# The middle term of a three-term fp32 split: 20 of its tiles by TensorE and ScalarE instead of VectorE

## The chip, the cores and the metric

The kernel runs on one core of a Trainium2 chip. Time is device microseconds (us) of the whole execution. Six executions of the kernel before are at hand, and one more that was profiled. The engines are named as in the profile: PE (TensorE, matmul), PEld (its weight load), DVE (VectorE), ACT (ScalarE), POOL (GpSimd) and SP (SyncE, which issues most DMAs).

## What is computed

A retention layer over 768 steps, for 4 batches and 8 heads of width 64, and behind it two matrix products with a SiLU between them:

```python
# attention: q, k, v are (4, 8, 768, 64)
gamma = 1.0 - 2.0 ** (-5.0 - np.arange(H))
for t in range(S):
    state = gamma * state + einsum('bhd,bhe->bhde', k[:, :, t], v[:, :, t])
    y[:, :, t] = scale * einsum('bhd,bhde->bhe', q[:, :, t], state)
x = y.transpose(0, 2, 1, 3).reshape(3072, 512)
# w_in is (512, 2048), w_out is (2048, 512)
h = x @ w_in
g = h * (1.0 / (1.0 + np.exp(-h)))
return g @ w_out
```

The weights come as 64-bit floating point numbers; the kernel makes 32-bit numbers of their two words itself.

## The kernel before

**Precision by three products.** The large products run in the format fp32r, which the kernel treats as narrower than fp32. So each operand t is split in three parts, each a plane of one tile: plane 0 is the high part H, t scaled by slightly less than one (HALF) and rounded; plane 1 the low part L; plane 2 the middle M, a sum of H and L in which one is scaled by EPS = 2^-12 or its inverse. The product H·H' + L·L' goes into one PSUM bank (ha, or oa), M·M' into another (hb, or ob), and the difference of the two, with ha scaled by ONE_E, is the product in nearly full precision. One product of 128 x 512 thus takes three passes: `product_in` issues eight matmuls into ha, four into hb. The M plane is read by the last four only.

**Units, groups, slices.** Time is cut in six chunks c of 128 steps; a unit n is one chunk of one batch, so that there are 24 units and units 4c to 4c+3 make group c of 512 columns of x. w_in is used in 16 slices f of 128 columns. `product_in(c, f)` makes ha and hb of slice f and group c; ScalarE copies ha out (L492), VectorE takes hb off (L493, "g"), ScalarE does SiLU (L494), and the result goes to device memory to be fetched again for the second half, which multiplies by w_out (L617 to L619).

**Visits.** `visit(m)` works on three units at once: it transposes k and q of unit m (kp, qp, L331; ScalarE copies them out, L333), makes scores and state sums of unit m-1 (sc, L347 and L357; VectorE: am L365, mid L373, qt L322, state L377) and the output y of unit m-2 (L389). `finish_y` then copies y out (ys, L424) and `split_x` splits it: H on ScalarE (L435), L (L436) and M (L437) on VectorE. The last eight matmuls of y wait for a token that GpSimd writes (`fence`, L305), and once per chunk GpSimd also scales a table gq (L278), which qt reads.

**Weights.** `take_w` converts one slice: ScalarE ca (L193), VectorE five to six steps (cs L195, ca L197, cs L200, cp L202, cp L204, cs L207), and `split_w` makes H on ScalarE (L117), L on VectorE (wil, L119) and ScalarE (L121), and M on VectorE (L122).

**Order.** TensorE's order is written out by hand: visits 0 to 9 with products (0, 0) and (0, 1) after visits 6 and 9, then pairs of products (group 0 and group 1 with one slice) with visits 10 to 13 between them, then more products. On the other engines a scheduler chooses the order, from its own estimate of times, and every engine then runs its queue in that fixed order. Group 2 (LATE) is used twice: it is split at once into a tile of its own, kept in device memory too, and split again later by `late_x`. PSUM has three banks for ha, hb and kp, handed out in turn by `turn`:

```python
    def turn(name):
        turns[0] += 1
        return ps_h.tile([128, 512], FP32, tag=f"h{turns[0] % 3}", name=name)
```

so that each user of a bank waits for the reader of the bank's user three turns before.

Of the kernel before, what the change touches and what calls it, by code (L numbers as in the profile page):

```python
# [12 lines left out]
FP32 = mybir.dt.float32  # L13
FP32R = mybir.dt.float32r
U32 = mybir.dt.uint32
AF = mybir.ActivationFunctionType
ALU = mybir.AluOpType
# [8 lines left out]
EPS = 2.0 ** -12  # L26
# [5 lines left out]
def kernel(  # L32
# [27 lines left out]
    nc = tc.nc  # L60
    B, H, S, D = q.shape
    DM, DF = moe_w_in.shape
    C = 128
    NC = S // C
    HP = H // 2
# [7 lines left out]
    scale = 1.0 / math.sqrt(D)  # L73
# [4 lines left out]
    def pool(name, bufs, **kw):  # L78
        return ctx.enter_context(tc.tile_pool(name=name, bufs=bufs, **kw))
# [4 lines left out]
    const = pool("const", 1)  # L84
    ld = pool("ld", 2)
    one = pool("one", 1)
# [17 lines left out]
    def w_slot(f, name):  # L104
        if f < NF - 4:
            return wpool.tile([128, 3, 512], FP32R, tag=f"w{f}", name=f"{name}{f}")
        if f == NF - 4:
            quads[name] = wpool.tile([128, 4, 3, 512], FP32R, tag="wq", name=f"{name}4")
        return quads[name][:, f - NF + 4]

    def split_w(f, w32, name, factor):

        w = w_slot(f, name)
        lo = conv.tile([128, 512], FP32, tag="wl", name=f"{name}l_{f}")
        after = held if f >= NF - 4 else evac
        with tc.issue_after(after[0]) if after else ExitStack():
            nc.scalar.activation(out=w[:, 0, :], in_=w32, func=AF.Copy, scale=HALF * factor)  # L117
        high = w[:, 0, :].bitcast(FP32)
        nc.vector.scalar_tensor_tensor(out=lo, in0=w32, scalar=factor, in1=high,  # L119
                                       op0=ALU.mult, op1=ALU.subtract)  # L120
        nc.scalar.activation(out=w[:, 1, :], in_=lo, func=AF.Copy, scale=1.0 / EPS)  # L121
        nc.vector.scalar_tensor_tensor(out=w[:, 2, :], in0=high, scalar=EPS, in1=lo,  # L122
                                       op0=ALU.mult, op1=ALU.subtract)
        return w


    units = [(c, b) for c in range(NC) for b in range(B)]
# [103 lines left out]
            load_w(n // 2)  # L231


    ident = const.tile([128, 128], FP32, tag="ident", name="ident")
    make_identity(nc, ident)

    lag = const.tile([128, C], FP32, tag="lag", name="lag")
    for o in range(2):
        part = lag[ts(o, D), :D]
        nc.gpsimd.iota(part, pattern=[[1, D]], base=0, channel_multiplier=-1,  # L240
# [4 lines left out]
    for j in range(2):  # L245
        for a in range(HP):
            evac[:] = [nc.scalar.activation(out=decay[:, j, a, :], in_=lag[:, :D],
                                            func=AF.Exp, scale=float(lg[2 * a + j])).ins]
# [34 lines left out]
    xt, kt, qt, am = {}, {}, {}, {}  # L283
# [10 lines left out]
    turns = [0]  # L294
# [4 lines that stand above are left out]
# [18 lines left out]
    def scale_q(n):  # L317
        c, b = units[n]
        if c > 0 and b == 0:
            next_chunk()  # L320
        t, g = (x if c > 0 else x[:, :, D:] for x in (qt[n], gq))
        nc.vector.tensor_tensor(out=t, in0=t, in1=g, op=ALU.mult)  # L322

    def stage_t(n):

        for name, to, bufs, src, tp in (
                ("kt", kt, 2, kqv["k"][n], turn(f"kp_{n}")),
                ("qt", qt, 3, kqv["q"].pop(n), banks("q", f"qp_{n}", 1)[:, 0])):
            tp = tp.rearrange("p (a t) -> p a t", a=HP)
            for a in range(HP):  # L330
                nc.tensor.transpose(tp[:, a, :], src[:, 2 * a : 2 * a + 2, :], ident)  # L331
            to[n] = one.tile([128, HP, C], FP32, tag=name, name=f"{name}_{n}", bufs=bufs)
            evac[:] = [nc.scalar.copy(out=to[n], in_=tp).ins]  # L333

    def score_tile(n):
        u = banks("s", f"sc_{n}")
        sc, sums = (u[:, :, ts(i, 4 * D)].rearrange("p o (a t) -> p o a t", a=HP)
                    for i in range(2))
        return sc, sums
# [39 lines left out]
    def stage_y(n):  # L379

        vs, amn, qtn = kqv["v"].pop(n), am.pop(n), qt.pop(n)
        states = steps_of.pop(n)
        yp = banks("y", f"y_{n}")[:, :, : 4 * D].rearrange("p o (a t) -> p o a t", a=HP)

        started, done, new = set(), [], []

        def product(a, o, j, lhsT, rhs):
            e = j ^ (a % 2)
            i = nc.tensor.matmul(yp[ts(e, D), o, a, :], lhsT=lhsT, rhs=rhs,  # L389
                                 start=(e, o) not in started, stop=True,  # L390
                                 skip_group_check=True).ins
            started.add((e, o))
            if new:
                fence(done[-1], i)
                new.clear()
            done.append(i)

        def scores():
            for a in range(HP):
                for o in range(2):  # L400
                    for j in range(2):
                        product(a, o, j, vs[ts(o, D), 2 * a + j, :], amn[ts(o, D), j, a, :])

        def states_with(part):

            new.extend([part] * part)
            for a in range(HP):
                for o in range(2):
                    j = o ^ part
                    if states[o] is not None:  # L410
                        product(a, o, j, states[o][ts(j, D), a, :], qtn[ts(j, D), a, ts(o, D)])

        return scores, states_with, yp

    def finish_y(n, yp):
        c, b = units[n]
        if b == 0:
            p, tag = (wpool, "wq") if c == LATE else (xpool, "xt")
            xt[c] = p.tile([128, 3, KIN, NT], FP32R, tag=tag, name=f"xt_{c}")
        raw = None  # L420
        if c <= LATE:

            raw = hpool.tile([128, KIN, C], FP32, tag="hs", name=f"ys_{n}")
            nc.scalar.copy(out=raw.rearrange("p a (o t) -> p o a t", o=2), in_=yp)  # L424
            if c == LATE:
                nc.sync.dma_start(out=y_dram[b], in_=raw)
        split_x(c, b, yp, raw)

    def split_x(c, b, y, raw):
        x = [xt[c][:, i, :, ts(b, C)] for i in range(3)]  # L430
        if raw is None:
            xh, xl = (t.rearrange("p a (o t) -> p o a t", o=2) for t in x[:2])
        else:
            (xh, xl), y = x[:2], raw
        held[:] = [nc.scalar.activation(out=xh, in_=y, func=AF.Copy, scale=HALF).ins]  # L435
        nc.vector.tensor_tensor(out=xl, in0=y, in1=xh.bitcast(FP32), op=ALU.subtract)  # L436
        nc.vector.scalar_tensor_tensor(out=x[2], in0=x[1].bitcast(FP32), scalar=-1.0 / EPS,  # L437
                                       in1=x[0].bitcast(FP32), op0=ALU.mult, op1=ALU.add)

    LATE = 2
# [8 lines left out]
    def visit(m):  # L451

        first, mid, last = (0 <= m - i < len(units) for i in range(3))
        if first:
            stage_t(m)
        if last:
            scores, states_with, yp = stage_y(m - 2)
            scores()
        if mid:
            sc, sums = score_tile(m - 1)  # L460
            stage_s(m - 1, sums)
        if last:
            states_with(0)
        if mid:
            stage_a(m - 1, sc)
            with tc.issue_after(taken_out[0]) if taken_out else ExitStack():
                finish_a(m - 1, sc, sums)
            scale_q(m - 1)
        if m == 0:
            chunk_decays()  # L470
            first_chunk()
        if first:
            scale_k(m)
        if last:
            states_with(1)
            finish_y(m - 2, yp)
        for name, n in (("k", m + 2), ("q", m + 2), ("v", m + 1)):
            if n >= EARLY:
                load(name, n)
# [2 lines left out]
    pending = []  # L482

    def product_in(c, f):
        ha, hb = turn(f"ha_{c}_{f}"), turn(f"hb_{c}_{f}")
        for i in range(3):
            for kk in range(KIN):
                nc.tensor.matmul(hb if i == 2 else ha, lhsT=w_sb[f][:, i, ts(kk, 128)],  # L488
                                 rhs=xt[c][:, i, kk, :], start=kk == 0 and i != 1,
                                 stop=kk == KIN - 1 and i != 0)  # L490
        hs = hpool.tile([128, NT], FP32, tag="hs", name=f"g_{c}_{f}")
        nc.scalar.activation(out=hs, in_=ha, func=AF.Copy, scale=ONE_E)  # L492
        taken_out[:] = [nc.vector.tensor_tensor(out=hs, in0=hs, in1=hb, op=ALU.subtract).ins]  # L493
        nc.scalar.activation(out=hs, in_=hs, func=AF.Silu)  # L494
        pending.append((c, f, hs))
# [102 lines left out]
    for c in range(NC):  # L598
# [8 lines left out]
        for f in range(NF):  # L607
            n = c * NF + f
# [3 lines left out]
            t = ready.pop(n)  # L612
# [7 lines left out]
        for b in range(B):  # L620
            oa, ob = acc[b]
            o = one.tile([128, DM], FP32, tag=("kt", "qt")[b % 2], name=f"o_{c}_{b}",
                         bufs=(2, 3)[b % 2])
# [33 lines left out]
```

## Time and profile before

| | us |
|---|---|
| median of 6 executions | 661.51 (658.46 to 663.4) |
| profiled execution, whole | 660.73 |
| its span, first to last instruction | 659.0 |
| PE busy | 618.8 |
| DVE busy | 428.4 |
| ACT busy | 288.5 |
| POOL busy | 15.2 |

The profile shows one execution. "Busy" is the time in which an engine had an instruction running; matmuls are pipelined, so a busy PE is not PE at its peak. The page's slices give the busy share of each of 40 equal parts of the span in tenths, and PEclk the clock that TensorE was granted, in tenths of full speed. In a group of instructions the columns are: line, engine, operation, output <- input, shape, count, then busy time and mean ns of one, then idle time of the engine just before them and what ended it. These are the groups that the change touches or copies:

```profile
L437 DVE SCALAR_TENSOR_TENSOR xt<-xt 128x512 fp32r<-128x512 f32 x28 | 19.2, 685 | 0.3
L122 DVE SCALAR_TENSOR_TENSOR wi<-wi,wil 128x512 fp32r<-128x512 f32 x16 | 11.0, 689 | 0.3
L492 ACT ACTIVATE g<-ha 128x512 f32<-128x512 f32 x96 | 56.5, 589 | 26.9 <-PE ha L488 24.1 <-ACT xt L435 1.6 <-DVE xt L436 0.8
```

### The profile page before, as it was taken

The numbers are of one execution on the slowest core, as the hardware profiler recorded it, in microseconds if no ns is written. First come the engines' busy times: TensorE is split into PE (matmuls) and PEld (weight loads), VectorE is DVE, ScalarE is ACT, GpSimd is POOL, SyncE is SP. The second block draws the span as 40 slices with busy tenths as digits, with TensorE's granted clock in tenths as the row PEclk, the third lists the DMA queues.
The fourth block names the chain that finished last, engine by engine and source line by source line (L and its number), as shares of the span: only waits on it lengthen the run. The fifth ranks groups of instructions, "written<-read, shape, count | busy, mean of one in ns | idle before, by whom it ended". The sixth has DMA issues, their size and how long they took to land.

```text
span 659.0 us, 13483 instructions
## 1 busy us (share of the span) xinstructions
PE 618.8 (94%) x5440; PEld 509.5 (77%) x5440; DVE 428.4 (65%) x736; ACT 288.5 (44%) x522; POOL 15.2 (2%) x70
## 2 busy tenths in 40 slices
PE   4787988999999899999989999999999999999996
PEld 3666867888878677888768888888888888888885
DVE  4888898966968877758858857455463545554631
ACT  5564655656646344445437863222131412222311
POOL 3002000000000000000000000000000000000000
PEclk9897998999999899999999999999999999999999
DMA  9995676553476865756746644242343332433301
GB/s 202 195 203 143 184 213 175 178 192 116 163 275 170 211 176 177 224 176 208 234 154 205 208 150 156 92 165 95 98 159 97 135 121 95 160 96 97 128 0 64
DMA packets 123070, 103.64 MB, mean 157 GB/s; under 512 B 80000, under 2 KB 88192, under 8 KB 123008
## 3 DMA queue, kind: packets, MB, share of 16 engines
q1 hardware_dynamic: 119552, 96.49, 49.9%
q10 hardware_dynamic: 3456, 6.29, 2.6%
q8 instruction: 42, 0.69, 0.4%
q14 instruction: 20, 0.16, 0.1%
HBM read 66.06 MB, written 36.70 MB: 156 GB/s over the span
## 4 chain that ended last, share of the span: by engine, by line
PE 72%; DVE 13%; DMA 5%; ACT 4%; issue 3%; SPq 3%; POOL 0%; ACTq 0%; DVEq 0%; POOLq 0%
PE ha L488 18%; PE hb L488 9%; PE ob L619 7%; PE o L619 7%; PE o L617 7%; PE oa L617 7%; PE o L618 7%; PE oa L618 7%; PE y L389 2%; DMA kqv<-in_q_dram 2%; SPq L145 2%; DVE g L493 2%; DVE cp L204 2%; DVE cs L200 1%; DMA wod<-cw 1%
## 5 line engine op out<-in xcount | busy, mean ns | idle before, releaser
L488 PE MATMUL ha<-xt,wi 128*128 128x512 f32 x768 | 195.2, 396 | 5.8 <-DVE g L493 4.2
L488 PEld LDWEIGHTS ha<-xt,wi 128*128 128x128 f32 x768 | 143.0, 189 | 39.9 <-DVE g L493 7.7
L539 DVE TENSOR_TENSOR gs<-gr,gs 128x512 fp32r<-128x512 f32 x96 | 62.1, 685 | 90.3 <-ACT gs L537 90.3
L537 ACT ACTIVATE gs<-gr 128x512 fp32r<-128x512 f32 x96 | 53.5, 621 | 134.2 <-issue 131.9
L488 PE MATMUL hb<-xt,wi 128*128 128x512 f32 x384 | 103.0, 390 | 1.2 <-ACT g L492 1.1
L493 DVE TENSOR_TENSOR g<-g,hb 128x512 f32<-128x512 f32 x96 | 65.6, 683 | 49.1 <-PE hb L488 40.3
L494 ACT ACTIVATE g<-g 128x512 f32<-128x512 f32 x96 | 60.6, 632 | 77.6 <-DVE g L493 76.7
L488 PEld LDWEIGHTS hb<-xt,wi 128*128 128x128 f32 x384 | 72.0, 188 | 17.1 <-ACT g L492 1.6
L619 PE MATMUL ob<-wo,gs 128*128 128x512 f32 x192 | 75.2, 392 | 0.0
L619 PE MATMUL o<-wo,gs 128*128 128x512 f32 x192 | 74.7, 389 | 0.0
L617 PE MATMUL o<-wo,gs 128*128 128x512 f32 x192 | 74.7, 389 | 0.0
L618 PE MATMUL o<-wo,gs 128*128 128x512 f32 x192 | 74.7, 389 | 0.0
L617 PE MATMUL oa<-wo,gs 128*128 128x512 f32 x192 | 74.7, 389 | 0.0
L618 PE MATMUL oa<-wo,gs 128*128 128x512 f32 x192 | 74.7, 389 | 0.0
L492 ACT ACTIVATE g<-ha 128x512 f32<-128x512 f32 x96 | 56.5, 589 | 26.9 <-PE ha L488 24.1
L540 DVE SCALAR_TENSOR_TENSOR gs<-gs 128x512 fp32r<-128x512 f32 x96 | 61.9, 683 | 0.0
L619 PEld LDWEIGHTS ob<-wo,gs 128*128 128x128 f32 x192 | 36.0, 188 | 8.9 <-DVE o L625 1.6
L618 PEld LDWEIGHTS o<-wo,gs 128*128 128x128 f32 x192 | 36.0, 188 | 7.6
L619 PEld LDWEIGHTS o<-wo,gs 128*128 128x128 f32 x192 | 36.0, 188 | 7.5
L618 PEld LDWEIGHTS oa<-wo,gs 128*128 128x128 f32 x192 | 36.0, 188 | 7.5
L617 PEld LDWEIGHTS oa<-wo,gs 128*128 128x128 f32 x192 | 36.0, 188 | 7.5
L617 PEld LDWEIGHTS o<-wo,gs 128*128 128x128 f32 x192 | 36.0, 188 | 7.2
(80 smaller groups left out, 652.5 us busy)
## 6 DMA issues: line engine op xcount, KB each, us to landing
gd<-g SPq DMA_DIRECT2D x96, 256.0 KB, 2.8
gr<-gd SPq DMA_DIRECT2D x96, 256.0 KB, 2.7
wf<-in_moe_w_out_dram SPq DMA_DIRECT2D x16, 512.0 KB, 4.2
out_dram<-o ACTq DMA_DIRECT2D x24, 256.0 KB, 2.1
wf<-in_moe_w_in_dram SPq DMA_DIRECT2D x16, 256.0 KB, 3.3
wf<-in_moe_w_in_dram SPq DMA_DIRECT2D x32, 128.0 KB, 3.6
kf<-in_k_dram SPq DMA_DIRECT2D x16, 256.0 KB, 5.2
qf<-in_q_dram SPq DMA_DIRECT2D x16, 256.0 KB, 4.6
```

The lines of the kernel that those rows point to most:

```text
L145: nc.sync.dma_start(out=t, in_=src[b, :, ds(c * C, C)].rearrange("h t d -> t h d"))
L204: nc.vector.scalar_tensor_tensor(out=p.bitcast(FP32), in0=lo, scalar=2.0 ** -52, in1=p.bitcast(FP32), op0=ALU.mult, op1=ALU.mult)
L488: nc.tensor.matmul(hb if i == 2 else ha, lhsT=w_sb[f][:, i, ts(kk, 128)], rhs=xt[c][:, i, kk, :], start=kk == 0 and i != 1, stop=kk == KIN ...
L492: nc.scalar.activation(out=hs, in_=ha, func=AF.Copy, scale=ONE_E)
L493: taken_out[:] = [nc.vector.tensor_tensor(out=hs, in0=hs, in1=hb, op=ALU.subtract).ins]
L494: nc.scalar.activation(out=hs, in_=hs, func=AF.Silu)
L537: nc.scalar.activation(out=t[:, 0, :], in_=g, func=AF.Copy, scale=HALF)
L539: nc.vector.tensor_tensor(out=t[:, 1, :], in0=g, in1=high, op=ALU.subtract)
L540: nc.vector.scalar_tensor_tensor(out=t[:, 2, :], in0=t[:, 1, :].bitcast(FP32), scalar=-1.0 / EPS, in1=high, op0=ALU.mult, op1=ALU.add)
L617: nc.tensor.matmul(oa, lhsT=gh, rhs=wo[f][:, 0, :], start=first_, stop=False)
L618: nc.tensor.matmul(oa, lhsT=glo, rhs=wo[f][:, 1, :], start=False, stop=last)
L619: nc.tensor.matmul(ob, lhsT=gm, rhs=wo[f][:, 2, :], start=first_, stop=last)
```

## The change

M of the 12 units of groups 0 to 2 (at their first split), and of the first eight slices of w_in, is no longer made by VectorE. `split_w` and `split_x` leave a function behind for each instead. Called later, it takes a PSUM bank by `turn`, multiplies H by the unit matrix and L by a unit matrix times -1 (w_in) or -1/EPS (x), both into that bank, and lets ScalarE write the bank to plane 2. The function is called at two places in TensorE's order: for unit m-3 at the end of visit m, and, right ahead of the product that needs them, for the slice f and for the last unit of the group. M of the other units, of the other eight slices, of w_out and of g stays on VectorE, as do the four of `late_x`.

The three matrices (`eyes`, fp32r) are written by GpSimd at the start from a unit matrix, and the transposes use the first of them. For the space, the unit matrix is built in a buffer of mid, and lag, a table of the start, moves into the buffer of am.

```diff
@@ split_w
-        nc.vector.scalar_tensor_tensor(out=w[:, 2, :], in0=high, scalar=EPS, in1=lo,
-                                       op0=ALU.mult, op1=ALU.subtract)
+        if name == "wi" and f < PE_MIDDLE:
+            middles["w", f] = lambda: middle(w[:, 2, :], w[:, 0, :], w[:, 1, :], 1, EPS)
+        else:
+            nc.vector.scalar_tensor_tensor(out=w[:, 2, :], in0=high, scalar=EPS, in1=lo,
+                                           op0=ALU.mult, op1=ALU.subtract)
         return w
+    middles = {}
+    PE_MIDDLE = 8
+
+    def middle(out, high, low, i, factor):
+        p = turn(f"mp_{turns[0]}")
+        p = p if len(high.shape) == 2 else p.rearrange("p (a t) -> p a t", a=HP)
+        for n, x in ((0, high), (i, low)):
+            nc.tensor.matmul(p, lhsT=eyes[:, n, :], rhs=x, start=n == 0, stop=n > 0)
+        nc.scalar.activation(out=out, in_=p, func=AF.Copy, scale=factor)
@@ constants
-    ident = const.tile([128, 128], FP32, tag="ident", name="ident")
-    make_identity(nc, ident)
-
-    lag = const.tile([128, C], FP32, tag="lag", name="lag")
+    eyes = const.tile([128, 3, 128], FP32R, tag="eyes", name="eyes")
+    eye = one.tile([128, 128], FP32, tag="mid", name="eye", bufs=2)
+    make_identity(nc, eye)
+    for i, x in enumerate((1.0, -1.0, -1.0 / EPS)):
+        nc.gpsimd.tensor_scalar(out=eyes[:, i, :], in0=eye, scalar1=x, scalar2=None,
+                                op0=ALU.mult)
+    ident = eyes[:, 0, :].bitcast(FP32)
+
+    lag = one.tile([128, C], FP32, tag="am", name="lag")
@@ finish_y, split_x
-        split_x(c, b, yp, raw)
+        split_x(c, b, yp, raw, n if c <= LATE else None)
-        nc.vector.scalar_tensor_tensor(out=x[2], in0=x[1].bitcast(FP32), scalar=-1.0 / EPS,
-                                       in1=x[0].bitcast(FP32), op0=ALU.mult, op1=ALU.add)
+        if n is not None:
+            middles["x", n] = lambda: middle(x[2], x[0], x[1], 2, 1.0)
+        else:
+            nc.vector.scalar_tensor_tensor(out=x[2], in0=x[1].bitcast(FP32),
+                                           scalar=-1.0 / EPS, in1=x[0].bitcast(FP32),
+                                           op0=ALU.mult, op1=ALU.add)
+
+    def finish_middle(*which):
+        middles.pop(which, lambda: None)()
@@ visit
             finish_y(m - 2, yp)
+        finish_middle("x", m - 3)
@@ product_in
     def product_in(c, f):
+        finish_middle("w", f)
+        finish_middle("x", (c + 1) * B - 1)
```

More of the change, by code (lines that the diff above doesn't have):

```diff
@@ L426, in finish_y, with split_x @@
                 nc.sync.dma_start(out=y_dram[b], in_=raw)
-        split_x(c, b, yp, raw)
-    def split_x(c, b, y, raw):
+        split_x(c, b, yp, raw, n if c <= LATE else None)
+    def split_x(c, b, y, raw, n=None):
         x = [xt[c][:, i, :, ts(b, C)] for i in range(3)]
```

## The prediction

> **What bounds the kernel now.** I read the page's busy times and slices first, then the busy time by stage, then the chain of waits and the timeline of the first 125 us, where the change lies.
>
> ```profile
> PE 618.8 (94%) x5440; PEld 509.5 (77%) x5440; DVE 428.4 (65%) x736; ACT 288.5 (44%) x522; POOL 15.2 (2%) x70
> ...
> PE   4787988999999899999989999999999999999996
> DVE  4888898966968877758858857455463545554631
> ...
> 39.40:75.30 35.90, 30.38 (x490) 25.16 (x483) 28.71 (x53) 19.69 (x34) 3.50 (x4) 0.90 0.64 156
> 75.30:112.30 37.00, 31.53 (x617) 26.17 (x615) 32.88 (x59) 21.46 (x40) 1.57 (x5) 0.95 0.73 201
> 112.30:190.00 77.70, 77.70 (x342) 64.00 (x343) 61.97 (x111) 48.57 (x83) 0.00 (x0) 1.00 0.54 181
> ```
>
> In the stage lines the columns are stretch, length, then PE, weight load, DVE, ACT, POOL, clock, DMA share and GB/s. After 112.3 us TensorE is busy in every us up to 190: there a matmul added is time added, and VectorE time saved is worth nothing. Between 39.4 and 112.3 us TensorE stands idle 5.5 + 5.5 us and its clock is 0.90 to 0.95. That is all there is to win in those two stages, plus what the low clock costs. What ends these idle times:
>
> ```profile
> PE kp L331 <- DVE g L493: 4.6, 3, 2.0
> PE y L389 <- POOL token L305: 2.5, 1, 2.5
> PE y L389 <- DVE am L365: 1.8, 1, 1.8
> ...
> 56.05 0.52 POOL gq L278
> 56.57 2.72 issue
> 59.29 0.10 POOL token L305
> ...
> 59.89 3.59 PE ha L488 x8
> ...
> 67.13 1.81 PE ha L488 x8
> ...
> 60.00:61.00 1.00, 1.00 (x3) 0.81 (x4) 0.40 (x2) 0.97 (x2) 0.00 (x0) 0.50 1.15 317
> ...
> 84.50 0.61 DVE g L493
> 85.11 0.04 issue
> 85.15 0.66 PE kp L331 x4
> ```
>
> Three visits (85.15, 95.50 and 107.56 us) wait for a PSUM bank that VectorE frees with g, L493, and at 85.15 and 95.50 an M of x (L437, at 83.81 and 94.16) is directly ahead of it in VectorE's timeline. The fourth wait is another thing: GpSimd's gq took 3.3 us at 56.05, 1.04 at 32.61 and 104.12. TensorE stood for 2.5 us, and then ran four us at clock 0.50: eight ha took 3.59 us at 59.89 against 1.81 at 67.13. Idle times of 1.24 and 1.33 us brought no low clock, those of 1.78 (at 46.7) and 2.02 us (at 105.5) did.
>
> [...] from 56.05 to 58.37 VectorE ran only instructions without a PSUM operand, and gq ended right after L365 and L373, which read PSUM; at 104.12 gq got in beside L377, which reads PSUM, and the next L436 took 1.42 us for 0.68. [...]
>
> **The change part by part.** Durations are of the profiled execution (span 659.0 us, 660.73 in all; 0.8 below the median of 661.51).
>
> VectorE loses 12 L437 and 8 L122. Back to back, such instructions follow each other at 0.60 us (83.21, 83.81, 84.42), so it is relieved of 20 x 0.60 = 12.0 us, most of it before 121 us. TensorE gains 40 matmuls 128x512 of the kind of ha, at 1.81 / 8 = 0.227 us: 9.1 us, 0.45 for each M. ScalarE gains 20 copies out of PSUM, by the row of L492 0.59 us: 11.8 us. It has room (44%), but it works strictly in its order. GpSimd gains three small scalings before 5 us, while TensorE waits for the first k until 6.8: nothing. The lag and eye buffers are free before am and mid are first written (15.2 us): nothing. Loads have the same order up to unit 9; afterwards some change places with stores; the one weight load in the chain here (92.83, 3.87 us) landed as VectorE's instruction before its reader ended: nothing, at worst half a us. A product of a diagonal with fp32r data is not in the trace; [...] at twice that the change would add 9 us more: I take 0.227.
>
> The order of the engines' instructions in the built kernels tells where things stand, and I follow TensorE through it.
>
> Up to 39.4 us. M of units 0 and 1 stands before visits 4 and 5, which wait for k and q (TensorE idle to 31.85): hidden. Unit 2 stands before visit 6 (0.45), unit 3 and slice 0 before the first product (0.9): that product is 1.35 us later. Its ScalarE copies lie under its eight ha (1.81).
>
> 39.4 to 59.9. The 1.35 goes through kp, the table load and the conversion of slice 2 to am (47.61, now 49.0). VectorE drops L437, but wil now waits for ScalarE after the last step of the conversion (0.85 of stall), and am of visit 9 comes at 55.0; y of that visit starts near 56.3, held by ys on ScalarE, which is queued behind wi<-wil. Then the gain: in the new order qt of unit 7 is followed by state (L377, a PSUM reader), as at 104.12, not by xt and kf. So gq [...] takes 1.04, and y goes on at 58.1 rather than 59.43. kf pays 0.7. M of unit 6 waits for its low part until 59.0, that of slice 1 follows, ha starts at 59.9 as before, but without the long idle time: at full clock. The product ends at 62.95, was 64.40: 1.45 ahead.
>
> To 75.3. M of unit 7 needs the low part of unit 7, which VectorE now does behind three more conversion steps, at 64.1: TensorE idle 1.2, and 0.45 for the M. M of slice 2 costs 0.45, and the next ha waits 0.65 for ScalarE, which has ha of (1, 1) behind wi<-cs. Sum -1.45 + 1.2 + 0.45 + 0.45 + 0.65, less 0.1 of rounding: visit 10 starts 1.2 late.
>
> Three rounds to 112.3. The cycle that sets their length is kp, qt copy, ca on ScalarE, ca on VectorE and eleven instructions to g. Two drop out (1.2 us), but only L437 stood ahead of g; in its place come wil (0.60) and the next cs (0.34). From ca to g it was 5.92 (88.84 to 94.76), and is 6.3. At the other end ca on ScalarE can be 0.1 to 0.4 earlier, as one conversion copy is gone from ahead of it. I get 9.6, 10.9 and 11.5 us per round, where 10.0, 10.35 and 12.06 were. Visit 13 starts at 108.3 (was 107.56). The M's here (0.45, 0.9, 0.9) lie in the wait for g, which was 1.2 to 2.0 us: free. If that cover were gone, 2.3 us.
>
> After that, M of unit 10 and slice 6 (0.9) brings ha of slice 6 to 112.3 if the shorter idle time leaves the clock up, to 113.8 if not. M of unit 11 waits for g, and ha of (2, 0) for the copy of ha behind wi<-wil on ScalarE: 120.3 instead of 117.96 in either case. M of slice 7 adds 0.45, and with some slack in the readings I have 2.5 us at slice 7. From there to 190 TensorE was and is the bound; all that follows moves by that amount.
>
> The sum: 660.7 + 2.5 = 663.2 against the profiled execution, 664.0 against the median.
>
> **The rivals.** First, faster: the relief of VectorE reaches g after all, and the three rounds fall to what TensorE itself needs, a visit of 3.05 to 3.3, one or two M of 0.45 and 5.44 of products: 9.0 + 9.7 + 9.7 = 28.4 against my 32.0. Then g is also there in time for (2, 0), which saves its 1.4: 664.0 - 3.6 - 1.4 = 659.0. It is faster from a sum of the rounds of about 28.9 on. For it: L437 stood right before g. Against: the built order puts two others there, and ca on ScalarE starts the cycle as late as before.
>
> Second, the full price. TensorE is busy 94%; if the waits stay, since ScalarE's new copies stand in them, 9.1 us come on top of 661.5: 670.6. For it: in ScalarE's built order copies of ha sit behind conversion copies that wait for VectorE, in each round. Against: three waits of 1.2 to 2.0 us are there to take them.
>
> Third, gain and price cancel: 661, with gq short and no wait at unit 7.
>
> **How the numbers follow.** The middle case (662 to 667) has 0.47, the full price (667 to 672) 0.18, cancelling (659.5 to 663) 0.18, the gain (656 to 659.5) 0.17. What can be told from no change is 0.3%, 2.0 us: 659.5 to 663.5. Slower: 0.40 of the middle and 0.18: 0.58. Same: 0.18 and the rest of the middle: 0.25. Faster: 0.17. Unknown costs: gq at 1.04 or 3.3 (2.3 us), each half clock 1.5 to 1.8, with two of them open, and the M at up to twice the price. The range is 657.5 to 670.6.
>
> **What would show it.** mp in x40 at 0.39 busy and 9.1 us between them; L437 x16 and L122 x24 (8 of them for w_in); gq at 1.04 near 57 us with clock 1.00 from 60 to 64; visit 13's kp near 108; ha of (2, 0) near 120; nothing different after 125 us but a shift. The forecast is wrong if gq again takes 3 us, if rounds are under 9 us, or if TensorE stands idle ahead of many of the mp.

## The result, and the profile after

The changed kernel takes 664.64 us (median of 17 executions, 662.28 to 667.33), the kernel before 661.33 us (36 executions, 657.42 to 665.37). The ratio is 1.0057, with a 95% interval of 1.0041 to 1.0072: slower by 3.3 us between the medians. The profiled execution took 663.48 us in all, 2.75 more than the profiled one of before, with a span of 661.7 us.

Lines of code have moved: what was L193 to L223 is now L207 to L237, L278 is L298, L305 is L325, L331 is L351, L435 to L437 are L455, L456 and L460, L488 and L492 to L494 are L518 and L522 to L524. The new matmuls are at L137, their copies at L138. First the page of the changed kernel, busy times and slices:

```profile
PE 624.7 (94%) x5480; PEld 513.6 (78%) x5480; DVE 418.4 (63%) x716; ACT 298.2 (45%) x542; POOL 14.2 (2%) x73
...
PE   4788998999999799999979999999999999999996
...
DVE  4769678965968967667857757464464545554631
```

VectorE has lost 10.0 us of busy time and ScalarE has gained 9.7, as the work was moved. Now the same three stages as before, in the same columns (stretch, length, then PE, weight load, DVE, ACT, POOL, clock, DMA share, GB/s):

```profile
39.40:75.30 35.90, 32.18 (x496) 26.03 (x495) 25.89 (x48) 23.56 (x42) 1.50 (x4) 0.95 0.64 165
75.30:112.30 37.00, 34.06 (x635) 28.28 (x634) 28.52 (x51) 23.66 (x44) 1.39 (x5) 1.00 0.71 189
112.30:190.00 77.70, 76.32 (x336) 62.45 (x335) 61.17 (x109) 49.78 (x87) 0.00 (x0) 1.00 0.51 173
```

In the first two stages TensorE is busy 1.8 and 2.5 us more, in the same time and at a higher clock (0.95 and 1.00 for 0.90 and 0.95). In the third it stands idle 1.4 us, where before it never did. TensorE's waits from 36 to 125 us, summed by what ended them (us in total, times, longest):

```profile
PE y L409 <- issue: 2.9, 3, 1.5
PE kp L351 <- DVE g L523: 2.2, 2, 1.8
PE hb L518 <- ACT wi L138: 1.3, 1, 1.3
...
PE ha L518 <- ACT g L522: 0.3, 1, 0.3
PE y L409 <- POOL token L325: 0.2, 1, 0.2
```

The wait for the token went from 2.5 to 0.2 us, that for g from 4.6 to 2.2. Waits of y for which the profile names no releaser (issue) went up from 0.8 to 2.9, and one wait is new: hb for a copy of M. All the waits that the view lists for this stretch are 8.0 us together, before 11.6, so idle time has taken in 3.6 of the 9.1 us of new matmuls. The timeline of ScalarE shows what stood ahead of that copy (wi<-mp, at 113.71):

```profile
111.66 0.67 ACT L207 ACTIVATE ca<-wf 128x512 f32<-128x512 f32 x1 [1.22 <-DVE cs L214]
112.23 0.57 ACT L444 COPY ys<-y 128x512 f32<-128x512 f32 x1
112.70 0.61 ACT L138 ACTIVATE xt<-mp 128x512 fp32r<-128x512 f32 x1
113.19 0.63 ACT L455 ACTIVATE xt<-ys 128x512 fp32r<-128x512 f32 x1
113.71 0.60 ACT L138 ACTIVATE wi<-mp 128x512 fp32r<-128x512 f32 x1
```

TensorE had issued that M and begun ha by 111.07. ScalarE ran these five in that order, and ca at their head waited 1.22 us for VectorE, so that the copy came at 113.71 and hb at 114.36.

I followed the start of each product through both traces. At slice 7 of group 0 (ha of (0, 7)) the changed kernel is 1.40 us behind. That stays so to 190 us. But then the two part again: by 213 us it has won back 0.4, a stretch of half clock near 218 us, which this trace doesn't have (1.00 from 218 to 221 us) and that of before does (0.50 from 217 to 220), gives it 1.45, and from 330 to 342 us it loses 3.2. The timeline of TensorE there, before:

```profile
332.41 1.07 PE L488 MATMUL hb<-xt,wi 128*128 128x512 f32 x4
335.14 2.11 PE L488 MATMUL ha<-xt,wi 128*128 128x512 f32 x8 [1.66 <-DVE g L493]
337.09 1.07 PE L488 MATMUL hb<-xt,wi 128*128 128x512 f32 x4
```

and after:

```profile
331.97 1.07 PE L518 MATMUL hb<-xt,wi 128*128 128x512 f32 x4
336.34 3.60 PE L518 MATMUL ha<-xt,wi 128*128 128x512 f32 x8 [3.31 <-DVE g L523]
339.78 1.09 PE L518 MATMUL hb<-xt,wi 128*128 128x512 f32 x4
```

The number in brackets is the idle time before. The wait for g is 1.65 us longer, and after it eight ha take 3.60 us in place of 2.11: the granted clock is 0.50 from 337 to 339 us, where before it is 1.00 from 333 to 342. VectorE is late there with the conversion of a slice of w_out, and by the profile the conversion waits for two transfers. The first is the load of the slice. On ScalarE the conversion begins with ca, which before came so:

```profile
327.54 0.66 ACT L193 ACTIVATE ca<-wf 128x512 f32<-128x512 f32 x1 [1.85 <-DMA wf<-in_moe_w_out_dram]
```

and after, where TensorE is 0.45 us ahead at this point:

```profile
327.74 0.67 ACT L207 ACTIVATE ca<-wf 128x512 f32<-128x512 f32 x1 [2.50 <-DMA wf<-in_moe_w_out_dram]
```

The second is the store of what was converted just before (wod<-cw), which is still on its way when VectorE is to write cw again. Before, cw did not wait:

```profile
328.57 0.68 DVE L207 TENSOR_TENSOR cw<-cs,cp 128x512 f32<-128x512 f32 x1
```

and after:

```profile
329.76 0.69 DVE L221 TENSOR_TENSOR cw<-cs,cp 128x512 f32<-128x512 f32 x1 [0.90 <-DMA wod<-cw]
```

Load and store were issued at the same place of TensorE's work as before (at 322.79 and 323.52 us, before at 323.24 and 323.97, always 0.45 apart). They took longer, though. The last number is us from issue to landing, before:

```profile
wf<-in_moe_w_out_dram SPq DMA_DIRECT2D x1, 512.0 KB, 4.2
wod<-cw SPq DMA_DIRECT2D x1, 256.0 KB, 4.2
```

and after:

```profile
wf<-in_moe_w_out_dram SPq DMA_DIRECT2D x1, 512.0 KB, 4.9
wod<-cw SPq DMA_DIRECT2D x1, 256.0 KB, 6.2
```

So the difference of the two profiles is +1.4 us near the change, +1.3 us far behind it. Is the second part of the change or of the single execution? And is the first the price of 20 M, or of a few of them?

### The profile page after: what moved, and what is told of

Read it like the earlier page. It is cut to its first block, busy times and chain, and to the rows that moved or that the text cites. A ratio compares the mean times of both kernels' runs of the same rounds, so it can differ in the third digit from the quotient of the medians.

```text
span 661.7 us, 13576 instructions
## 1 busy us (share of the span) xinstructions
PE 624.7 (94%) x5480; PEld 513.6 (78%) x5480; DVE 418.4 (63%) x716; ACT 298.2 (45%) x542; POOL 14.2 (2%) x73
## 4 chain that ended last, share of the span: by engine, by line
PE 70%; DVE 14%; ACT 5%; DMA 4%; issue 3%; SPq 3%; ACTq 0%; DVEq 0%; POOLq 0%; POOL 0%
PE ha L518 17%; PE hb L518 8%; PE ob L649 7%; PE o L647 7%; PE oa L647 7%; PE o L649 7%; PE o L648 7%; PE oa L648 7%; DVE g L523 2%; DVE cs L214 2%; PE y L409 2%; DVE cp L218 2%; SPq L159 2%; DMA wod<-cw 1%; DVE xt L456 1%
## 5 line engine op out<-in xcount | busy, mean ns | idle before, releaser
L518 PE MATMUL ha<-xt,wi 128*128 128x512 f32 x768 | 194.5, 395 | 7.8 <-DVE g L523 5.9
L518 PEld LDWEIGHTS ha<-xt,wi 128*128 128x128 f32 x768 | 143.5, 189 | 42.3 <-DVE g L523 8.8
L518 PE MATMUL hb<-xt,wi 128*128 128x512 f32 x384 | 103.2, 391 | 2.2 <-ACT wi L138 1.3
L524 ACT ACTIVATE g<-g 128x512 f32<-128x512 f32 x96 | 60.6, 631 | 77.6 <-DVE g L523 76.8
L518 PEld LDWEIGHTS hb<-xt,wi 128*128 128x128 f32 x384 | 71.8, 188 | 18.9 <-ACT wi L138 2.1
L522 ACT ACTIVATE g<-ha 128x512 f32<-128x512 f32 x96 | 56.6, 590 | 22.7 <-PE ha L518 18.5
```

## The experiments

Five theories. A: the cost is local, and the last of the moved M make it (units 10 and 11, slices 6 and 7), since they stand where TensorE is bound. B: it is the far wait. C: each M costs the same. D, formed after the first four runs: moving M of x is free because its new order also shortens gq, and M of w_in has nothing to pay with. E, formed with D: M of w_in pays its full length on TensorE. All ratios are to the kernel before on the same chip.

**The changed kernel again**, with no edit.

> The changed kernel as it is, to see what of its trace comes back in another execution. Theory A (the cost is local: the last of the moved M, of units 10 and 11 and of slices 6 and 7, stand on a bound TensorE and behind ScalarE's order): ha of (0, 7) again near 122.2 us, 1.4 later than in the kernel before, and this is in every execution. Theory B (the cost is far off: the shifted times make the wait for g at 336 us longer): the wait of 3.3 us at 336 and the half clock after it come back too. If the wait at 336 is 1.7 us this time while the time stays 0.5% above the kernel before, B falls. Time 664.6, ratio 1.004 to 1.007.

665.45 us (17 executions), ratio 1.0074 (1.0053 to 1.0095). From the first product to ha of (0, 7) this trace loses 1.47 us against the first one of before, as the first trace of it did (1.42). The far wait came back too: 3.24 us, with both transfers late again (ca waits 2.42 us for its load, cw 0.92 for the store), and the half clock behind it: from the start of ha to that of hb it is 3.38 us, 3.44 in the first trace and 1.95 before. So both parts came back. Other things vary: the first product started 0.6 us later, and the half clock near 218 us was there this time (32 matmuls of y took 1.02 us there, 0.69 in the first trace).

**M of x alone, and M of w_in alone.**

```diff
@@ x_alone
-    PE_MIDDLE = 8
+    PE_MIDDLE = 0
@@ w_alone
-        split_x(c, b, yp, raw, n if c <= LATE else None)
+        split_x(c, b, yp, raw)
```

> Only M of x by TensorE (12 of 20 moved M); M of w_in is VectorE's as before. A: of the last four M two are left (units 10 and 11): 0.9 us of TensorE and the wait for the copy behind ScalarE's order in part, so +0.7 to +1.5 us against the kernel before. Theory C (each moved M costs the same, 3.3 us / 20 = 0.17 us, wherever it stands): +2.0 us. B: either 0 or +3, by whether the wait at 336 us is long.

> Only M of the first eight slices of w_in by TensorE (8 of 20). A: of the last four M slices 6 and 7 are left; VectorE keeps 12 M of x of which three stand straight ahead of g: +0.7 to +1.5 us. C: 8 x 0.17 = +1.3 us. B: 0 or +3, by the wait at 336 us.

x_alone: 660.64 us, ratio 0.9996 (0.9972 to 1.0019). w_alone: 665.39 us, ratio 1.0062 (1.0041 to 1.0084). Twelve M cost nothing, eight cost 4 us: C falls. Neither shows the far wait of the changed kernel: it is 1.88 us in x_alone and 1.51 in w_alone, and cw waits for no store. The traces show one thing that goes with the difference in time. GpSimd's gq near 55 us, with M of x moved:

```profile
55.60 1.04 POOL L298 TENSOR_TENSOR gq<-gq,step 128x512 f32<-128x512 f32 x1 [4.91 <-DVE qt L342]
```

and with only M of w_in moved:

```profile
55.00 3.29 POOL L298 TENSOR_TENSOR gq<-gq,step 128x512 f32<-128x512 f32 x1 [3.84 <-DVE qt L342]
```

**Without the last four M.**

```diff
-    PE_MIDDLE = 8
+    PE_MIDDLE = 6
-        split_x(c, b, yp, raw, n if c <= LATE else None)
+        split_x(c, b, yp, raw, n if n < 10 else None)
```

> The changed kernel with M of units 10 and 11 and of slices 6 and 7 left to VectorE, so 16 M of 20 by TensorE. A: the cost is gone, ha of (0, 7) at 120.8 us or up to 1 us before it, time 0 to 1.5 us under the kernel before (659.8 to 661.3 where that has 661.3), so a ratio to the kernel before of 0.998 to 1.000. C: 16 x 0.17 = +2.6 us, ratio 1.004. B: time by the wait at 336 us alone, within 0.5 us of the changed kernel if the wait is long.

664.19 us, ratio 1.0043 (1.0026 to 1.0061). A is wrong as the whole cause. The trace loses 1.56 us between the first product and ha of (0, 7), as much as the changed kernel, but in another place: ha of (2, 0) now waits 1.7 us for g. The far wait is 2.79 us.

**The kernel before again.**

> The kernel before as it is, one more profile, to see what of its trace is fixed. Stage from the first product to 190 us: within 0.3 us of the first profile (the changed kernel's two profiles agree there to 0.03 us). gq again 3.3 us near 56 us. If the wait at 335 us comes out at 1.7 us and no half clock follows, Theory B (the far wait is longer in the changed kernel by a fixed amount) stays alive; if it is over 2 us or the clock halves there this time too, B falls.

This single execution took 656.92 us, less than any of the 62 that the first four runs were compared with (657.24 to 665.47). Its trace shows where 2.9 us of it come from; 0.9 more lie ahead of the first product. The timeline of the first profile of before, GpSimd's line and below it VectorE's:

```profile
56.05 3.30 POOL L278 TENSOR_TENSOR gq<-gq,step 128x512 f32<-128x512 f32 x1 [4.63 <-DVE qt L322]
...
55.28 0.68 DVE L322 TENSOR_TENSOR qt<-qt,gq 128x512 f32<-128x512 f32 x1
55.89 0.68 DVE L436 TENSOR_TENSOR xt<-ys,xt 128x512 fp32r<-128x512 f32 x1
56.49 0.68 DVE L315 TENSOR_TENSOR kf<-kf,gk 128x512 f32<-128x512 f32 x1
```

and the second:

```profile
55.19 1.49 POOL L278 TENSOR_TENSOR gq<-gq,step 128x512 f32<-128x512 f32 x1 [4.83 <-DVE qt L322]
...
54.42 0.69 DVE L322 TENSOR_TENSOR qt<-qt,gq 128x512 f32<-128x512 f32 x1
55.09 0.69 DVE L436 TENSOR_TENSOR xt<-ys,xt 128x512 fp32r<-128x512 f32 x1
55.69 1.53 DVE L315 TENSOR_TENSOR kf<-kf,gk 128x512 f32<-128x512 f32 x1
```

The order is the same, and yet gq was done in 1.49 us beside kf the second time (kf is stretched from 0.68 to 1.53), and the first time its 3.30 us ran over kf, not stretched, and four more instructions. The second execution is 2.9 us faster from the first product to ha of (0, 7), and by 392 us nothing but 0.05 us has been added to that: the far wait was 1.62 us, and no half clock behind it shows in that sum. So the far difference (B) comes back: 1.66 and 1.62 us in two traces of the kernel before, 3.31 and 3.24 in two of the changed one. And the kernel before has a reserve of some 3 us that an execution can draw or not.

**Only the order that frees gq.** For unit 7 state is issued behind qt; no M is moved. The scheduler moves a few conversion steps behind it as well. The same edit was made to w_alone.

```diff
@@ finish_a
-                nc.vector.tensor_tensor(out=state[b], in0=mid, in1=sums[:, 1], op=ALU.add)
+                def add(out=state[b], mid=mid, sums=sums):
+                    nc.vector.tensor_tensor(out=out, in0=mid, in1=sums[:, 1], op=ALU.add)
+                if n == 2 * B - 1:
+                    adds.append(add)
+                else:
+                    add()
@@ scale_q
-        nc.vector.tensor_tensor(out=t, in0=t, in1=g, op=ALU.mult)
+        i = nc.vector.tensor_tensor(out=t, in0=t, in1=g, op=ALU.mult).ins
+        while adds:
+            with tc.issue_after(i):
+                adds.pop()()
```

> The kernel before with one change of order: for unit 7, state (L377, reads PSUM) is issued on VectorE after qt instead of ahead of it, so that gq meets an instruction that reads PSUM soon after it may start; no M is moved. Theory D (moving M of x is free because its new order also frees gq, and moving M of w_in has nothing to pay with): gq takes 1.0 to 1.6 us, the 2.5 us wait for the token at 59 us falls under 1 us and ha of (0, 1) runs at full clock; time 2 to 4 us under the kernel before, ratio 0.994 to 0.997. Theory A or C with gq of no consequence: 0.998 to 1.002.

> w_alone with the same change of order for unit 7. D: gq falls from 3.29 to 1.04 us, time 2 to 4 us under w_alone (665.4), so 661.4 to 663.4, ratio to the kernel before 1.000 to 1.003. If gq does not matter: as w_alone, 1.006.

before_port: 657.41 us, ratio 0.9954 (0.9933 to 0.9975). By its median it is the fastest kernel of this study, ahead of both. Its gq took 1.42 us, and at ha of (0, 7) its trace is 2.4 us ahead of the first one of before, counted from the first product. The second trace of before, with the old order and a short gq, is 2.9 ahead there, so a short gq is enough for a gain of this size, without the conversion steps that moved. w_port: 663.65 us, ratio 1.0045 (1.0023 to 1.0067), 1.7 us under w_alone where 2 to 4 were expected, gq 1.04. D holds for the kernel before; for w_alone the intervals overlap, so there it is only likely. Set against before_port, the changed kernel pays 7.2 us for its 20 M, x_alone 3.2 for 12, w_port 6.2 for 8. The three matrices and the moved buffers of the start are in these numbers too; they were not run alone.

**M of w_in twice on TensorE.** The edit is made to w_alone.

```diff
-        for n, x in ((0, high), (i, low)):
+        for n, x in ((0, high), (i, low)) * 2:
```

> w_alone with each M of w_in made twice on TensorE (4 matmuls in place of 2, the same result), 16 more matmuls or 3.6 us. Theory E (M of w_in stands on a bound TensorE and pays its full length, nothing of the relief of VectorE comes back): +2.9 to +3.6 us over w_alone, ratio to the kernel before about 1.011. If its cost is instead the wait for ScalarE's copies or a far wait, the added matmuls lie beside these in part: +0 to +2 us, ratio 1.006 to 1.009.

665.27 us, ratio 1.0066 (1.0044 to 1.0089): nothing over w_alone, where E wanted at least 2.9. E falls for the whole time. In the traces w_double does lose 1.7 us more than w_alone from the first product to 190 us, half of the 3.6 added. But behind 190 us w_alone loses 2.3 us more and w_double nothing. That was between 189 and 207 us: a wait of hb of 1.90 us at 201.57 (0.45 in w_double), and behind it a low clock, 0.63 from 202 to 206 us (1.00 in w_double). w_port, with the same loss there, shows ScalarE behind a reload of x:

```profile
197.29 0.63 ACT L464 ACTIVATE xt<-yr 128x512 fp32r<-128x512 f32 x1 [2.58 <-DMA yr<-yd]
198.73 0.60 ACT L531 ACTIVATE g<-ha 128x512 f32<-128x512 f32 x1 [0.81 <-DVE xt L465]
```

In before_port the same copy waited 1.47 us for its reload. Behind 190 us the traces of this study lose between -0.2 us (w_double) and 4.6 (w_port) against the first one of before, though no M is moved there. I read it as a matter of when the transfers meet these waits; that is not shown. Of the 7.7 us by which w_port's trace falls behind that of before_port from the first product on, 3.0 lie between 190 and 208 us, so its 6.2 us are not the price of the M at their own places alone.

**M of x without units 10 and 11.** x_alone with `n if n < 10 else None` in the call of `split_x`.

> x_alone without units 10 and 11, so M of x of units 0 to 9 by TensorE and everything else by VectorE; gq stays short (state stands behind qt of unit 7). In x_alone's trace 4 us were lost between 114 and 121 us, at M of unit 11 (waits for VectorE) and at the ha after it. If those two M are the price of x (theory A, for x alone): the 3.2 us between x_alone (660.6) and before_port (657.4) go, time 657 to 658.5. If each M costs alike (C): 660.1. If VectorE or ScalarE set the end of this stretch at about 121 us anyway: 659 to 660.5.

659.03 us, ratio 0.9971 (0.9955 to 0.9987), 1.6 us under x_alone, in which these lines stood where the four us were lost:

```profile
115.00 0.73 PE L137 MATMUL mp<-xt,eyes 128*128 128x512 f32 x2 [0.51 <-DVE g L523]
116.94 3.08 PE L518 MATMUL ha<-xt,wi 128*128 128x512 f32 x8 [1.20 <-ACT g L522]
```

In x_ten TensorE's waits from 110 to 125 us are 0.2 us in all, and the slow product (3.08 us for eight ha; 1.98 at clock 1.00 in the changed kernel, at 59.62 us) is gone. The 1.6 us are half of the 3.2 that A wanted, and just inside what was expected if the end of this stretch is set in another way: ha of (0, 7) comes at 120.89 us where x_alone has 121.39. x_alone had been 3.2 us ahead of x_ten at slice 6 and lost that lead again. The intervals of the two kernels overlap.

**All M twice on TensorE, and all copies twice on ScalarE.**

```diff
@@ after_double
-        for n, x in ((0, high), (i, low)):
+        for n, x in ((0, high), (i, low)) * 2:
@@ after_copies
-        nc.scalar.activation(out=out, in_=p, func=AF.Copy, scale=factor)
+        for _ in range(2):
+            nc.scalar.activation(out=out, in_=p, func=AF.Copy, scale=factor)
```

> The changed kernel with each of the 20 M made twice on TensorE (the same result): 40 more matmuls, 9.1 us. If TensorE's time is what the change pays (C, and the rival of the full price): +5 to +9 us over the changed kernel, about 671. If it is not, the most of it lies in waits as it did for w_double (+0 over w_alone): +0 to +2.5 us, about 666.

> The changed kernel with each of the 20 copies out of PSUM on ScalarE made twice (the same result): 20 more copies, 11.8 us, in ScalarE's order. If the change pays in ScalarE's order (hb and ha that wait for a copy): +3 to +8 us over the changed kernel, 668 to 673, with more waits of hb on wi and of ha on g. If ScalarE's room (45% busy) takes it: +0 to +1.5 us.

after_double: 673.4 us, ratio 1.0185 (1.0149 to 1.0220), 8.8 us over the changed kernel for 9.1 us of matmuls. after_copies: 672.73 us, ratio 1.0172 (1.0137 to 1.0208), 8.1 us for 11.8 us of copies. My low expectation from w_double was wrong for the first. TensorE's waits from 36 to 125 us in after_double:

```profile
PE hb L518 <- ACT wi L138: 4.0, 4, 1.5
PE sc L377 <- issue: 3.6, 2, 1.8
PE y L409 <- DVE am L385: 0.6, 1, 0.6
```

The line of kp and g is not there any more; in after_copies it is 0.2 us. The waits for g that had taken in a part of the first 20 M (4.6 us before, 2.2 left in the changed kernel) are used up, and a second set of M is paid nearly in full on TensorE, and by two thirds on ScalarE. In both, hb waits four or five times for the copy of M of w_in (4.0 and 5.0 us in all): matmuls and copy stand one behind the other ahead of it.

**The long gq put back.** In the changed kernel, qt of unit 7 is issued behind state again.

```diff
@@ scale_q
-        nc.vector.tensor_tensor(out=t, in0=t, in1=g, op=ALU.mult)
+        with tc.issue_after(state_at[0]) if n == 2 * B - 1 else ExitStack():
+            nc.vector.tensor_tensor(out=t, in0=t, in1=g, op=ALU.mult)
```

> The changed kernel with the order of unit 7 put back as it was before: qt behind state on VectorE, so that seven instructions without a PSUM operand follow qt [...]. If the changed kernel owes a gain to its new order (theory D: the 20 M cost about 7 us, the short gq gives some 3.5 back): gq of 3 to 4.5 us near 56 us, y waits 2 us or more for the token, time 2.5 to 5 us over the changed kernel, 667 to 669.5. If gq does not matter in the changed kernel: 664 to 665.5.

665.59 us, ratio 1.0075 (1.0049 to 1.0102): as the changed kernel. But it didn't do what it was made for:

```profile
56.18 1.42 POOL L298 TENSOR_TENSOR gq<-gq,step 128x512 f32<-128x512 f32 x1 [5.22 <-DVE qt L344]
...
56.01 0.69 DVE L459 TENSOR_TENSOR xt<-ys,xt 128x512 fp32r<-128x512 f32 x1
56.62 1.27 DVE L209 TENSOR_SCALAR cs<-wf 128x512 uint32<-128x512 uint32 x1
```

gq was done in 1.42 us beside cs, which reads nothing from PSUM and was stretched to 1.27 us (0.42 in the median in the changed kernel). So this run tells nothing on what the changed kernel would take with a long gq.

## Why the prediction was right, and where it was not

The time was 664.64 us where 664.0 was predicted, and the sum of 2.5 us on the profiled execution was 2.75. The sum held; its parts did not all hold, and that two of them erred in opposite directions, so that the sum came out right, is luck.

- The counts and durations held: a copy took 0.594 to 0.598 us (0.59 predicted), an M on TensorE 0.56 and 0.47 us (110.04, 110.60, ha at 111.07) for 0.45, and the second set in after_double made the kernel 8.8 / 20 = 0.44 us slower for each M. A diagonal product lasts as long as one of ha: 0.40 us (x) and 0.39 (w_in) in the median, ha 0.39 before.
- "gq at 1.04 near 57 us": it took 1.04 us in both traces of the changed kernel (at 55.25 us in the first), the wait for the token behind it is gone (the 0.2 us left are at 50.99 us, in an earlier visit), and ha of (0, 1) started at 59.62 (59.9 predicted) at clock 1.00, 1.98 us for eight. Right. What I didn't know is that the gain is over one outcome of the kernel before, which is not fixed: its gq took 3.30 us in one execution and 1.49 in another. That before_port is 3.7 us faster than before suggests that the long one is the usual case, as I had assumed without saying it.
- "Unit 3 and slice 0 before the first product": 1.35 us predicted. The first product came at 39.41 and 40.03 us, before at 39.43 and 38.57. The scatter of the start is as large as the term; it can't be told.
- "TensorE idle 1.2" at M of unit 7, and 0.65 at ha of slice 2: no idle time at the first, 0.28 at the second. So visit 10 started 0.15 us early, not 1.2 late. These two waits are the step that failed near the change: 1.85 us predicted together, 0.28 measured, a difference larger than the local error of 1.1 us.
- The rounds: 9.6, 10.9 and 11.5 us predicted, 9.63, 10.79 and 11.53 measured. Taking L437 from ahead of g is made good by what the order puts in its place, as the step had it. Whether the clock would hold after visit 13's wait was left open: it did, 1.00 from 107 to 112 us in both traces (the wait was 1.78 us in the first), where before it was 0.63 from 108 to 112 (2.02 us).
- ha of (2, 0) waits for ScalarE, due at 120.3: it came at 118.81, after a wait of 1.3 us of hb, for a copy of M, at slice 6, which I had not seen. At slice 7 it was 1.40 us instead of 2.5.
- "Nothing different after 125 us but a shift": wrong, and the largest error. In two of two traces the changed kernel loses 3.0 to 3.2 us between 330 and 342 us. The local term was 1.1 us too high and the far term, taken as nothing, at least 1.3 too low (2.8 in the second trace, where the clock did halve near 218 us). In the first trace the two errors cancel. The cause of the far term is known as far as two transfers, load and store of w_out, that are issued at the same place and take 0.7 and 2.0 us longer. Why they do is open. Far waits of 2.7 us and more stand only in traces of kernels that move M of both kinds (after, after_again, early_ones, after_copies, after_long; after_double has 2.16). The five that move one kind have 1.51 to 2.02 us.

Of the rivals, the full price (9.1 us) was nearer to the mechanism than I gave it credit for: beside before_port the change pays 7.2 us. The gain that I had booked for gq is what made the price look small, and it needed no moved M at all. The two faces of it, that M of w_in pays more than M of x, have a reading in the order of VectorE: L437 stands ahead of g and L122 behind it (106.23, 106.83 and 107.43 us in the first trace), so that only the first gives something back. That is argued, not shown, and in the changed kernel itself two other instructions stand in L437's place (L119 and L209, at 105.14 and 105.85 us, with g at 106.19).

## What to carry to other kernels

Ask of a moved instruction what its new order frees by the way, and run that order alone: here it was worth 3.7 us, more than anything that the moved work gave. Ask of a relieved engine whether the instruction that goes stood ahead of the one that others wait for, and what the new order puts in its place. The idle time of the bound engine can be spent once (here it took in 3.6 of 9.1 us, and the second set of M cost 8.8 of 9.1); doubling the moved work shows in one run whether any is left. Where a kernel has waits for transfers far behind the change, as much can be made or lost there as in the changed stretch (here 3.0 to 3.2 us at one place), so a sum over the changed stretch is not the whole sum.

## What the runs showed of the hardware that was not expected

- The same order of instructions gave a GpSimd instruction of 3.30 us in one execution and of 1.49 in another. In before_again and after_long gq ran beside the instruction that followed the one in progress when it started: kf (1.53 us for 0.68) and cs (1.27 for 0.42), neither of which reads PSUM. In the first trace of before it didn't: kf, cs and ca followed, at 0.68, 0.41 and 0.41 us, and gq ended at 59.35. So a PSUM reader behind it is one way to a short gq, not the only one, as the prediction's reading had it. What decides between the two outcomes is not shown.
- Half clock after an idle time: at the far wait, in 14 traces, idle times of 1.51 to 1.66 us (four traces) brought none, those of 1.79 to 3.31 us (ten) all did, and the product behind it took 1.3 to 2.4 us longer. But the length alone does not decide. TensorE also waits near 218 us, for 2.57 to 2.61 us in each of the 14 traces; eleven have a half clock behind it, and three (after, early_ones, w_double) have none. The same wait before, with the clock at 0.50 from 217 to 220 us, and after, with 1.00 from 218 to 221:

```profile
216.84 1.14 PE L389 MATMUL y<-am,vf 64*64 64x64 f32 x32 [2.60 <-DVE xt L436]
...
217.84 0.69 PE L409 MATMUL y<-am,vf 64*64 64x64 f32 x32 [2.60 <-DVE xt L456]
```

What else decides is not shown: a single wait of 1.79 us was enough at the far place (before_port), and 2.6 us at the other was enough in eleven traces and not in three. Two executions of the changed kernel differ by 1.44 us at this one wait (after and after_again).
